# Score blocks of a slot on different rows of the array, P.V products in every second step, and exponentials in a ring of fifteen blocks

## The chip, the cores and the metric

The kernel runs on one core of one Trainium2 chip. The metric is the device time of one execution in microseconds (us), less is better. The median of three runs of the kernel before is 852.49 us (851.96 to 856.82).

## What is computed

A gated mix of two branches over the same 2048 tokens of width 640, all in bf16: softmax attention with 32 heads of width 20, and a dense layer with a Mish activation and 1536 hidden columns.

```python
g = sigmoid((x * gate_w).sum(-1, keepdims=True))

# branch A: attention, H = 32 heads, Dh = 20
qkv = (x @ wqkv).reshape(B, S, 3, H, Dh).transpose(2, 0, 3, 1, 4)
q, k, v = qkv[0], qkv[1], qkv[2]
p = softmax(einsum("bhqd,bhkd->bhqk", q, k) * Dh ** -0.5, axis=-1)
a = einsum("bhqk,bhkd->bhqd", p, v).transpose(0, 2, 1, 3).reshape(B, S, D) @ wo

# branch B: dense, Mish, dense
h = einsum("bsd,df->bsf", x, w1) + b1
sp = log1p(exp(-abs(h))) + where(h > 0, h, 0)
b = einsum("bsf,fd->bsd", h * tanh(sp), w2)

out = g * a + (1 - g) * b
```

## The kernel before

**Blocks.** The scores are computed transposed: keys on the partitions, 512 queries in the free direction. A *block* is one head's scores of 128 keys against 512 queries, one PSUM bank. Four heads with consecutive numbers form a head group `g` (there are 8) and lie on the 32-row strips `j` = 0 to 3 of `QT` and `KT`, so that score products of different `j` use different rows of the array (`tile_position=(32 * j, 0)`). With 4 chunks of queries `c` and 16 tiles of keys `kt` there are 4 x 8 x 16 x 4 = 2048 blocks. The last group is cut into two halves of 256 queries.

**Slots and steps.** A *slot* holds up to three blocks, in PSUM banks 0 to 2 (even slots) or 3 to 5 (odd ones). The main loop makes one *step* per slot. In step s ScalarE takes the exponential of slot s in one instruction (`emit_e`, L1086); then the scores of slot s + 2 are composed and emitted (`compose`, `emit_s`, `score_mms`, L1048), P.V products follow (`emit_pv`, `pv`, L1242), and last come *projections*: all products of the dense branch, of the QKV projection and of the output projection, taken from a list of tasks with due times (`pick`, `put`). Projections write to bank 7; when much of that work is owed (`now["rate"] > LEND`), odd slots hold only two blocks and lend bank 5 to projections as well (`lend`). The score products of slot s + 2 wait until slot s has been read.

**Blocks on VectorE.** Some slots carry an *extra*: their last block does not go to ScalarE. VectorE turns it into an approximate exponential in float16 bits, with a multiply and add that writes int16 (`emit_x`, L1117). The four heads of one key tile form a *tile* of four extras in four slots; when all four are in, VectorE makes three shifted copies (`SHADES`, L1137), and all four versions enter the P.V sum, so such a tile has four P.V sets in place of one. `choose` decides whether a slot gets an extra, by VectorE's backlog (`BEHIND`), by the fixed work that VectorE still owes (`room`, `LOAD`), and by free lines for the copies. `block_of` picks a block of the tile on a row that the slot's other two blocks don't use, if the tile has one left.

**P.V.** A *set* of P.V is the four heads of one key tile, four products of 21 columns side by side in the array (`tile_position=(0, 32 * j)`), summed in bank 6 over the whole group. `emit_pv` is called in each step and emits up to two sets of ScalarE blocks, and before each of them up to two sets of VectorE tiles (`emit_off`). When a group's last set is done, `group_done` copies the sum out and normalises it, and `hold` keeps P.V back for two steps.

**Where exponentials are kept.** `ETS` has five places (`NETS`) of three blocks (`SLOT`); slot s writes place s % 5, and waits for the P.V products of slot s - 5.

**What sets the order.** All five engines' instruction lists are written in one pass by a planner in the kernel's Python (`Plan`). It keeps an estimated time for each engine (`pl.now`), adds the cost given with each instruction (a change of the kind of product on TensorE adds `SWITCH`), and decides by these times; the constants at the top are its costs and thresholds. On the chip each engine runs its list in order, with semaphore waits between engines. A second program for inputs with very large scores follows behind a flag; it does not run with these inputs.

Of the kernel before, what the change touches and what calls it, by code (L numbers as in the profile page):

```python
# [13 lines left out]
AF = mybir.ActivationFunctionType  # L14
# [4 lines left out]
S = 2048  # L19
# [5 lines left out]
HG = 4  # L25
# [9 lines left out]
SCALE = DH ** -0.5  # L35
EW = DH + 1
NETS = 5
SLOT = 3
# [21 lines left out]
RECIP = 1.66  # L60
BLOCK = 0.43
STEP = 1.1
SLACK = 0.21
LATER = 0.616
FREE = 0.2
RISK = {"pe": 0.1, "act": 0.3, "dve": 0.5, "pool": 1.2, "sp": 0.6}
AHEAD = 16
BEHIND = 11.984
MORE = 5.931
PATIENCE = 1.785  # L70
CATCH_UP = 361.25
BUSY = 0.449
CROWD = 1.4
MARGIN = 0.575
EAGER = 26
LOAD = 0.786
MISH = 2.3
GROUP = 2.66
LAST = 0
OVER = 0.233  # L80
XSLACK = 0.336
BROAD = 1.13
LEND = 0.199
BEND = -0.21302449
QUART = (1.268632, -0.12838686 / 0.0119972, 0.72980421 / 0.0119972)
LEAD = 0.0119972
END = 83
SHIFT = 0.492
LAG = 200
WINDOW = 4.087  # L90
CALM = 4
PACKED = 13
Q_AT = 100
Q_STEP = 14.5
SQ = 25
SQ_STEP = 13
H_AT = 150
H_STEP = 12.5
# [122 lines left out]
def bass_gated_mix__softmax_full_mha__dense_activation_mish__prompt_kernel(  # L221
# [111 lines left out]
    def scores(s):  # L333
        return PS[:, SLOT * (s % 2):SLOT * (s % 2 + 1), :]

    NSLOT = -(-NC * NG * NKT * HG // SLOT)


# [3 lines left out]
    def attention(pl, fast):  # L342
# [7 lines left out]
        soon = deque()  # L350
        norm = deque()
        acts = deque()
        now = {"step": -1, "at": -2, "open": None, "home": FB, "bank": False, "rate": 9.0, "lent": False}


        if fast:
# [75 lines left out]
        def issue(task, bank):  # L432

            deps = []
            if task.done == 0:
                deps = [*task.ready(), bank_free.get(bank)]
            fn = task.mms[task.done]
            task.done += 1
            op = pl.add("pe", lambda e: fn(e, bank), deps, cost=task.cost)
            if task.done == len(task.mms):  # L440
                now["bank"] = True
                bank_free[bank] = task.finish(bank, op)
                now["bank"] = False
                return True
            return False
# [556 lines left out]


        s_op, e_op = {}, {}
        pv_slot, pv_left = {}, {}
        ev_op = {}
        taken, newest = set(), [-1]
        line_free = {("l", n): [] for n in range(LINES - fast)}
# [10 lines left out]
        def compose(s, extra=None):  # L1019

            n = SLOT - (s % 2 and now["lent"])
            if extra:
                slots[s] = [order.popleft() for _ in range(min(n - 1, len(order)))] + [extra]
            else:
                slots[s] = [order.popleft() for _ in range(min(n, len(order)))]
            now["at"] = (len(units) - len(order)) // SLOT - 2

        def emit_s(s):
# [9 lines left out]
        def score_mms(s, some, deps):  # L1038

            op = None  # L1040
            for r in range(max(len(subs(*u[:3])) for u in some)):
                began = False
                for i, (c, g, kt, j) in enumerate(some):
                    if r >= len(subs(c, g, kt)):
                        continue
                    tile, cols, of_q = subs(c, g, kt)[r]
                    cost = max(extent(c, g)[1] * COL, THIN)
                    op = pl.add("pe", lambda e, i=i, g=real(g), tile=tile, j=j, cols=cols, c=c, of_q=of_q: e.matmul(  # L1048
                        scores(s)[:, i, cols], KT[32 * j:32 * j + 32, g, tile * P:(tile + 1) * P],
                        QT[32 * j:32 * j + 32, g, c * CW:(c + 1) * CW][:, of_q], start=True, stop=True,  # L1050
                        tile_position=(32 * j, 0)), deps, cost=0.004 if began else cost, kind="S")
                    began, deps = True, []
            return op

        def repeat_s(s):
# [18 lines left out]
        def emit_e(s):  # L1074
            n = len(slots[s])
            by_dve = fast and s in off
            if by_dve:
                n -= 1
            while pv_left.get(s - NETS):

                hold["until"] = 0
                emit_pv(now["step"], 99)
                if pv_left[s - NETS]:
                    flush(lambda: emit_off(queue[0][2][:2], True, True))
                    emit_pv(now["step"], 99)
            e_op[s] = pl.add("act", lambda e: e.activation(  # L1086
                ETS[:, s % NETS, 0:n, :], scores(s)[:, 0:n, :], AF.Exp, scale=SCALE),
                [s_op[s], pv_slot.get(s - NETS)], cost=wide(s))
            pv_left[s] = n
            queue.extend((s, i, u) for i, u in enumerate(slots[s][:n]))  # L1090

# [68 lines left out]

        def choose(s, start):

            js = [v[3] for v in islice(order, 2)]
            late = max(0.0, pl.now["dve"] - pl.now["act"])
            urgent, other = (sum(t[0] for todo in some for t in todo) for some in ((norm, soon), (blend, bg)))
            tile = tile_now[0]
            if tile:
                if order and order[0][:2] == tile["key"][:2] and late + urgent + other >= BEHIND + MORE:
                    return None
                off[s] = block_of(tile, js)  # L1170
                return off[s][1]
            need = sum(len(SHADES) - len(t["items"]) for t in unshaded)
            if (not start or len(order) < 4 * HG or late + urgent + other >= BEHIND
                    or len(spare()) < 1 + min(need, len(SHADES) - 1)):
                return None
            c, g = group = order[2][:2]
            mine = [v for v in islice(order, 80) if v[:2] == group]
            left = (len(mine) - HG) * BLOCK
            before = sum(t[0] for t in blend if t[3] < pl.now["act"] + left)
            work_left = late + urgent + before + (len(SHADES) - 1) * SHADE  # L1180
            kts = [kt for kt in range(tiles(c, g)) if sum(v[2] == kt for v in islice(order, 2, 80) if v[:2] == group) == HG]
            if (len(kts) < 2 or 4 * EXP_PAIR + work_left * CROWD + MARGIN >= left
                    or newest[0] > place[group]):
                n = place[group] + 1
                if n >= len(groups):
                    return None
                c, g = group = groups[n]
                kts = [kt for kt in range(2) if (c, g, kt) not in taken]
                need = [k_done.get((real(g), 0)), q_done.get((real(g), c))]
                if not kts or any(op is None or safe(op) > pl.now["pe"] for op in need):  # L1190
                    return None
            key = (c, g, kts[0])
            taken.add(key)
            newest[0] = place[group]
            for j in range(HG):
                order.remove((*key, j))
            act_left[group] -= HG
            at, deps = grab()
            tile_now[0] = tile = {"key": key, "at": at, "deps": deps, "left": list(range(HG)), "seen": 0,
                                  "items": [], "given": 0, "shaded": None, "read": None}  # L1200
            off_tiles.setdefault(group, []).append(tile)
            off[s] = block_of(tile, js)
            return off[s][1]
# [41 lines left out]
                        cost=0.004 if n else max(w * COL, THIN), kind="V")  # L1245
            return lasts

        def emit_pv(step, passes):

            while passes and step >= hold["until"]:  # L1250
                if not queue:
                    return
                c, g, kt, _ = queue[0][2]
                emit_off((c, g), False)
                if len(queue) < HG:
                    return
                final = act_left[(c, g)] == HG
                if final and not emit_off((c, g), True):
                    if order or step + 1 in slots:
                        return  # L1260
                    flush(lambda: emit_off((c, g), True, True))
                passes -= 1
                some = [queue.popleft() for _ in range(HG)]
                lasts = pv([(u, ETS[:, s % NETS, i, :], [e_op[s]]) for s, i, u in some], final)
                act_left[(c, g)] -= HG
                for k, (s, i, u) in enumerate(some):
                    op = pv_slot[s] = lasts[k]
                    pv_left[s] -= 1
                if final:
                    hold["until"] = step + PV_HOLD  # L1270
                    group_done(c, g, step, op)
# [162 lines left out]
        def pick(limit):  # L1434
# [5 lines left out]
            begin = max(pl.now["pe"] + switch, free.t1 + HOP + FREE if free is not None else 0)  # L1440
            passed = False
            for t in tasks:
                if begin + t.cost > limit or passed and t.due > now["at"] + EAGER:
                    return None
                more = t.ready()
                passed = passed or more is None
# [81 lines left out]
        while True:  # L1528
# [41 lines left out]
                if fast and step + 2 in off:  # L1570
                    emit_x(step + 2)
            busy = order or step + 1 in slots
            emit_pv(step, 2 if busy else 99)

            limit = pl.now["act"] + wide(step + 1) + HOP + OVER if busy else 1e9
            owed = min(owed + rate, 1.0) if busy else 1e9
            while owed > 0:
                t = pick(limit)
# [180 lines left out]
```

## Time and profile before

| | |
|---|---|
| median of the runs | 852.49 us |
| profiled execution | 852.54 us, of which 850.2 us are the span from first to last instruction |
| TensorE matmuls (PE) | 832.1 us, 98% of the span |
| ScalarE (ACT) | 817.7 us, 96% |
| VectorE (DVE) | 701.8 us, 83% |
| TensorE weight loads (PEld) | 286.0 us, 34% |
| GpSimd (POOL) | 15.2 us, 2% |
| DMA | 42.58 MB, 50 GB/s on average |
| granted TensorE clock | 0.999 |

In the lines shown below, `L1086` is line 1086 of the kernel; `out<-in` are the program's names of the tiles written and read. A row of the groups of instructions ends with count, busy time and mean duration of one in ns, and, behind the last bar, the idle time of the engine ahead of them and what ended it. A row of the waits names who waited, for whom, the total in us, the number of times and the longest. A row in order of time begins with start and length in us and merges neighbours of one kind; its count is the number of instructions. A row of a stretch gives its length and each engine's busy time and, in brackets, count. Matmuls are pipelined, so the length of one is not what it adds to the time.

### The profile page before, as it was taken

The page shows a single profiled execution, that of the slowest core. Times are in us where ns is not written, and L with a number is a line of the kernel's source. Part 1 is how long each engine was busy: PE and PEld are TensorE (multiplying, and loading weights), DVE is VectorE, ACT ScalarE, POOL GpSimd, SP SyncE. Part 2 cuts the span into 40 slices and gives each one's busy share as a digit, 9 for nine tenths or more (in the row PEclk, how much of TensorE's full clock was granted, in tenths as well). Part 3 has the DMA queues.
Part 4 walks back from the last instruction along what each step waited for, and adds up shares of the span by engine and source line. Part 5 has one row for each costly group of instructions (what it writes and reads, how often), then busy time and mean ns, then how long its engine had stood idle before and what let it go on. Part 6 is the DMA issues. An engine that isn't in the chain of part 4 may idle for free.

```text
span 850.2 us, 17518 instructions
## 1 busy us (share of the span) xinstructions
PE 832.1 (98%) x7405; PEld 286.0 (34%) x7405; DVE 701.8 (83%) x1097; ACT 817.7 (96%) x848; POOL 15.2 (2%) x29
## 2 busy tenths in 40 slices
PE   8999999999999999999999999999999999999996
PEld 3333333233323333223333333333333333333332
DVE  4578776888798898987688999997999999998775
ACT  6999999999999999999999999999999999999995
POOL 3000000000000000000000000000000000000000
PEclk9999999999999999999999999999999999999999
DMA  9112110111112201131211121201112212000001
GB/s 216 40 52 52 58 38 3 35 55 48 30 55 81 62 31 42 33 106 41 48 50 48 51 72 43 64 22 37 47 58 60 77 39 74 17 26 25 15 15 35
DMA packets 70021, 42.58 MB, mean 50 GB/s; under 512 B 20616, under 2 KB 65920, under 8 KB 69888
## 3 DMA queue, kind: packets, MB, share of 16 engines
q1 hardware_dynamic: 67568, 40.89, 17.3%
q8 instruction: 61, 1.00, 0.5%
q10 hardware_dynamic: 2256, 0.47, 0.3%
q0 software_dynamic: 112, 0.01, 0.2%
q14 instruction: 24, 0.20, 0.1%
HBM read 33.97 MB, written 5.23 MB: 46 GB/s over the span
## 4 chain that ended last, share of the span: by engine, by line
PE 86%; ACT 10%; DMA 2%; SPq 1%; issue 0%; DVE 0%
PE PS L1048 32%; PE PS L1242 24%; ACT ETS L1086 9%; PE PS L901 7%; PE PS L840 7%; PE PS L547 5%; PE PS L925 4%; PE PS L722 2%; PE PS L601 2%; DMA XB<-in_A_x_dram 1%; SPq L478 1%; PE PS L763 1%; DMA REG<-in_B_w_dram 1%; PE PS L695 1%; PE PS L620 0%; ACT REG L874 0%
## 5 line engine op out<-in xcount | busy, mean ns | idle before, releaser
L1086 ACT ACTIVATE ETS<-PS 128x1024 bf16<-128x1024 f32 (+1 forms) x817 | 791.8, 1047 | 17.0 <-PE PS L1048 8.5
L1048 PE MATMUL PS<-QT,KT 32*128 32x512 bf16 (+1 forms) x2112 | 357.4, 377 | 6.6 <-ACT ETS L1086 5.3
L1117 DVE TENSOR_SCALAR LN<-PS 128x512 int16<-128x512 f32 x300 | 206.2, 687 | 72.8 <-PE PS L1048 68.4
L1242 PE MATMUL PS<-ETS,V_all 128*21 128x512 bf16 (+1 forms) x1720 | 163.7, 377 | 1.0 <-ACT ETS L1086 0.9
L1048 PEld LDWEIGHTS PS<-QT,KT 32*128 32x128 bf16 x2112 | 81.7, 91 | 230.6 <-ACT ETS L1086 130.5
L1137 DVE TENSOR_SCALAR LN<-LN 128x2048 int16<-128x2048 int16 x183 | 122.4, 684 | 0.5
L1242 PE MATMUL PS<-LN,V_all 128*21 128x512 f16 (+1 forms) x1300 | 111.8, 377 | 0.0
L901 PE MATMUL PS<-W2R,HB 128*128 128x320 bf16 x384 | 76.9, 303 | 0.0
L1242 PEld LDWEIGHTS PS<-ETS,V_all 128*21 128x21 bf16 x1720 | 42.1, 89 | 73.7 <-issue 64.3
L840 PE MATMUL PS<-XB,REG 128*128 128x256 bf16 x360 | 58.1, 275 | 0.4 <-DMA REG<-in_B_w_dram 0.4
L925 PE MATMUL PS<-WOQ,QT 128*128 128x320 bf16 x256 | 52.4, 303 | 0.0
L547 PE MATMUL PS<-XB,WOQ 128*128 128x512 bf16 x155 | 49.1, 384 | 0.0
L901 PEld LDWEIGHTS PS<-W2R,HB 128*128 128x128 bf16 x384 | 30.0, 97 | 44.7 <-issue 38.8
L1242 PEld LDWEIGHTS PS<-LN,V_all 128*21 128x21 bf16 x1300 | 25.9, 89 | 52.9 <-issue 27.8
L840 PEld LDWEIGHTS PS<-XB,REG 128*128 128x128 bf16 x360 | 28.6, 97 | 30.0 <-issue 26.4
L1117 DVE TENSOR_SCALAR REG<-PS 128x512 int16<-128x512 f32 x44 | 30.2, 686 | 7.5 <-PE PS L1048 6.7
L850 DVE TENSOR_TENSOR HB<-PS,B1F 128x512 bf16<-128x512 f32 x48 | 32.8, 684 | 2.9 <-PE PS L840 2.8
L925 PEld LDWEIGHTS PS<-WOQ,QT 128*128 128x128 bf16 x256 | 20.2, 97 | 29.6 <-issue 25.3
L893 DVE SCALAR_TENSOR_TENSOR U<-U 128x1024 f32<-128x1024 f32 x24 | 29.0, 1210 | 0.0
L559 DVE CAST QT<-PS 128x512 bf16<-128x512 f32 x31 | 21.3, 686 | 7.6 <-PE PS L547 7.2
L722 PE MATMUL PS<-REG,XB 128*128 128x160 bf16 (+1 forms) x240 | 26.0, 234 | 0.0
L1313 DVE COPY OUNG<-PS 128x512 f32<-128x512 f32 x31 | 21.3, 687 | 5.2 <-PE PS L1242 5.1
(113 smaller groups left out, 525.9 us busy)
## 6 DMA issues: line engine op xcount, KB each, us to landing
REG<-in_B_w_dram SPq DMA_DIRECT2D x36, 320.0 KB, 3.2
BCT<-SUMS SPq DMA_DIRECT2D x31, 256.0 KB
W2R<-in_B_w_dram SPq DMA_DIRECT2D x12, 320.0 KB, 4.7
KT<-KS SPq DMA_DIRECT2D x28, 128.0 KB
KS<-LN SPq DMA_DIRECT2D x16, 128.0 KB, 1.7
W2R<-in_B_w_dram SPq DMA_DIRECT2D x1, 1920.0 KB, 9.9
out_dram<-REG SPq DMA_DIRECT2D x24, 80.0 KB, 1.6
REG<-in_A_wqkv_dram SPq DMA_DIRECT2D x2, 700.0 KB, 8.3
```

What stands on the lines that cost most here:

```text
L547: return lambda e, bank: e.matmul(PS[:, bank, :], pads[:, b, f, :], xt(c)[:, f, :], start=(f == 0), stop=(f == NFT - 1))
L722: return lambda e, bank: e.matmul(PS[:, bank, i * n:(i + 1) * n], xt(t // 4)[:, f, t % 4 * P:(t % 4 + 1) * P], WV[:, f, g * HD:g * HD + n] ...
L840: return lambda e, bank: e.matmul(PS[:, bank, i * HW:(i + 1) * HW], w1b(n1)[:, f, i * P:(i + 1) * P], xt(c)[:, f, cols], start=(f == 0), s ...
L850: ev = dve(lambda e: e.tensor_tensor(hb, PS[:, bank, :].rearrange("p (i t) -> p i t", i=2), bias, ALU.add), [last, *b1f, *guarded, *b_read ...
L893: piece(BROAD, lambda e: e.scalar_tensor_tensor(G, G, b, G, ALU.add, ALU.mult))
L901: return lambda e, bank: e.matmul(PS[:, bank, 0:HALF], HB[:, hc % 2, f, t * P:(t + 1) * P], W2[:, f, half * HALF:(half + 1) * HALF], start ...
L925: return lambda e, bank: e.matmul(PS[:, bank, 0:HALF], otn(c, g)[:, t * P:(t + 1) * P], WOG[:, g, half * HALF:(half + 1) * HALF], start=(g ...
L1048: op = pl.add("pe", lambda e, i=i, g=real(g), tile=tile, j=j, cols=cols, c=c, of_q=of_q: e.matmul(scores(s)[:, i, cols], KT[32 * j:32 * j ...
L1086: e_op[s] = pl.add("act", lambda e: e.activation(ETS[:, s % NETS, 0:n, :], scores(s)[:, 0:n, :], AF.Exp, scale=SCALE), [s_op[s], pv_slot.g ...
L1117: ev_op[s] = tile["op"] = dve(lambda e: e.tensor_scalar(dst, scores(s)[:, 2, :], SCALE * ULPS, BASE, ALU.mult, ALU.add), [s_op[s], *tile[" ...
L1137: op = pl.add("dve", lambda e: e.tensor_scalar(to, src, SHADES[n], None, ALU.add), [last, *deps], cost=SHADE)
L1242: lasts[n] = pl.add("pe", lambda e, tile=tile, h=real(g) * HG + j, j=j, src=src[:, cols], of_q=of_q, begin=begin, end=end: e.matmul(PS[32 ...
```

## The change

- `compose` fills a slot block by block: an extra is placed first, and each next block is one from the first key tile of `order` that lies on a row not yet used in the slot, if there is one. The extra still comes last in the slot. `choose` tells `block_of` the rows of all blocks that remain of the first key tile, or none if more than two remain.
- Exponentials are written to a ring (`RING`, the same memory as `ETS`, 15 blocks); a slot takes as many blocks as it has, and waits for the P.V products of whichever slots own these blocks.
- `emit_pv` is called only in odd steps (`TURN`), unless `tight` holds (one of the next `ROOM` blocks of the ring is still unread, the oldest set is the group's last, or nothing else is to come) or `VMIN` sets are ready. Unless `tight`, it stops at the planner's `limit` for the step.
- A projection that begins a piece needs `FMIN` of room; each projection product is costed `MORE_MM` higher.
- Constants of the planner have other values.

```diff
-SLACK = 0.21
-LATER = 0.616
+SLACK = 0.225
+LATER = 0.659
-BEHIND = 11.984
+BEHIND = 44.659
-PATIENCE = 1.785
-CATCH_UP = 361.25
-BUSY = 0.449
+PATIENCE = 2.856
+CATCH_UP = 413.595
+BUSY = 0.437
-EAGER = 26
-LOAD = 0.786
+EAGER = 62
+LOAD = 1.258
-GROUP = 2.66
+GROUP = 2.418
-LEND = 0.199
+FMIN = 0.25
+VMIN = 11.592
+ROOM = 4.229
+TURN = 1
+MORE_MM = 0.005
+LEND = 0.139
-END = 83
-SHIFT = 0.492
-LAG = 200
+END = 33
+SHIFT = 0.481
+LAG = 186
-CALM = 4
+CALM = 10
-SQ = 25
+SQ = 32
...
+    NRING = NETS * SLOT
+    RING = ETS[:, :, :, :].rearrange("p a b c -> p (a b) c")
...
-        op = pl.add("pe", lambda e: fn(e, bank), deps, cost=task.cost)
+        op = pl.add("pe", lambda e: fn(e, bank), deps, cost=task.cost + MORE_MM)
...
         def compose(s, extra=None):
             n = SLOT - (s % 2 and now["lent"])
-            if extra:
-                slots[s] = [order.popleft() for _ in range(min(n - 1, len(order)))] + [extra]
-            else:
-                slots[s] = [order.popleft() for _ in range(min(n, len(order)))]
+            some = [extra] if extra else []
+            while len(some) < n and order:
+                js = [u[3] for u in some]
+                mates = [u for u in islice(order, HG) if u[:3] == order[0][:3]]
+                u = next((u for u in mates if u[3] not in js), mates[0])
+                order.remove(u)
+                some.append(u)
+            slots[s] = some[1:] + some[:1] if extra else some
...
         def emit_e(s):
-            while pv_left.get(s - NETS):
+            p = now["ring"] if now["ring"] + n <= NRING else 0
+            before = {owner.get(i) for i in range(p, p + n)} - {None}
+            while any(pv_left[b] for b in before):
                 hold["until"] = 0
                 emit_pv(now["step"], 99)
...
             e_op[s] = pl.add("act", lambda e: e.activation(
-                ETS[:, s % NETS, 0:n, :], scores(s)[:, 0:n, :], AF.Exp, scale=SCALE),
-                [s_op[s], pv_slot.get(s - NETS)], cost=wide(s))
+                RING[:, p:p + n, :], scores(s)[:, 0:n, :], AF.Exp, scale=SCALE),
+                [s_op[s], *(pv_slot[b] for b in before)], cost=wide(s))
+            spot[s] = p
+            owner.update({i: s for i in range(p, p + n)})
+            now["ring"] = (p + n) % NRING
...
         def choose(s, start):
-            js = [v[3] for v in islice(order, 2)]
+            js = [v[3] for v in islice(order, HG) if v[:3] == order[0][:3]]
+            if len(js) > 2:
+                js = []
...
+        def pressed():
+            at = now["ring"]
+            return any(pv_left.get(owner.get((at + i) % NRING)) for i in range(int(ROOM)))
+
-        def emit_pv(step, passes):
-            while passes and step >= hold["until"]:
+        def emit_pv(step, passes, limit=1e9):
+            while passes and step >= hold["until"] and pl.now["pe"] + PASS <= limit:
...
             for t in tasks:
-                if begin + t.cost > limit or passed and t.due > now["at"] + EAGER:
+                if begin + (t.cost if pl.kind == "F" else max(t.cost, FMIN)) > limit or passed and t.due > now["at"] + EAGER:
                     return None
...
             busy = order or step + 1 in slots
-            emit_pv(step, 2 if busy else 99)
             limit = pl.now["act"] + wide(step + 1) + HOP + OVER if busy else 1e9
+            tight = not fast or not busy or pressed() or queue and act_left[queue[0][2][:2]] == HG <= len(queue)
+            if tight or step % 2 == TURN or sets() >= VMIN:
+                emit_pv(step, 2 if busy else 99, 1e9 if tight else limit)
```

More of the change, by code (lines that the diff above doesn't have):

```diff
@@ L352, in attention @@
         acts = deque()
-        now = {"step": -1, "at": -2, "open": None, "home": FB, "bank": False, "rate": 9.0, "lent": False}
+        now = {"step": -1, "at": -2, "open": None, "home": FB, "bank": False, "rate": 9.0, "lent": False, "ring": 0}
         if fast:
@@ L1004, in attention @@
         s_op, e_op = {}, {}
-        pv_slot, pv_left = {}, {}
+        pv_slot, pv_left, spot, owner = {}, {}, {}, {}
         ev_op = {}
@@ L1041, in score_mms @@
             for r in range(max(len(subs(*u[:3])) for u in some)):
-                began = False
+                rows = set()
                 for i, (c, g, kt, j) in enumerate(some):
@@ L1050, in score_mms @@
                         QT[32 * j:32 * j + 32, g, c * CW:(c + 1) * CW][:, of_q], start=True, stop=True,
-                        tile_position=(32 * j, 0)), deps, cost=0.004 if began else cost, kind="S")
-                    began, deps = True, []
+                        tile_position=(32 * j, 0)), deps, cost=0.004 if rows and j not in rows else cost, kind="S")
+                    rows.add(j)
+                    deps = []
             return op
@@ L1078, in emit_e @@
                 n -= 1
-            while pv_left.get(s - NETS):
+            p = now["ring"] if now["ring"] + n <= NRING else 0
+            before = {owner.get(i) for i in range(p, p + n)} - {None}
+            while any(pv_left[b] for b in before):
                 hold["until"] = 0
                 emit_pv(now["step"], 99)
-                if pv_left[s - NETS]:
+                if any(pv_left[b] for b in before):
                     flush(lambda: emit_off(queue[0][2][:2], True, True))
@@ L1246, in pv, with sets @@
             return lasts
-        def emit_pv(step, passes):
-            while passes and step >= hold["until"]:
+        def sets():
+            if not queue:
+                return 0
+            n = len(queue) // HG
+            for tile in off_tiles.get(queue[0][2][:2], ()):
+                n += sum(op.t1 + HOP <= pl.now["pe"] for op, _ in tile["items"][tile["given"]:])
+            return n
+        def pressed():
[3 more added lines that the diff above has]
+            while passes and step >= hold["until"] and pl.now["pe"] + PASS <= limit:
                 if not queue:
@@ L1263, in emit_pv @@
                 some = [queue.popleft() for _ in range(HG)]
-                lasts = pv([(u, ETS[:, s % NETS, i, :], [e_op[s]]) for s, i, u in some], final)
+                lasts = pv([(u, RING[:, spot[s] + i, :], [e_op[s]]) for s, i, u in some], final)
                 act_left[(c, g)] -= HG
```

## Prediction

> **What bounds the kernel now.** I read the page's header first, then the waits, then ScalarE's and TensorE's instructions in order of time.
>
> ```profile
> span 850.2 us, 17518 instructions
> PE 832.1 (98%) x7405; PEld 286.0 (34%) x7405; DVE 701.8 (83%) x1097; ACT 817.7 (96%) x848; POOL 15.2 (2%) x29
> PE 86%; ACT 10%; DMA 2%; SPq 1%; issue 0%; DVE 0%
> PEld PS L1048 <- ACT ETS L1086: 130.5, 346, 0.9
> DVE LN L1117 <- PE PS L1048: 68.4, 112, 2.0
> ACT ETS L1086 <- PE PS L1048: 8.5, 34, 1.1
> PE PS L1048 <- ACT ETS L1086: 5.3, 21, 0.5
> ```
>
> Two engines look full, TensorE at 98% and ScalarE at 96%. The chain of work that ended last (third line) runs 86% on TensorE, but a busy share can hide waiting inside. The waits (last four) say that TensorE's score matmuls stood still for ScalarE only 5.3 us in all; the 130.5 us of the first are the weight loads, which are issued ahead and wait in the shadow of running matmuls. VectorE waits for TensorE's scores. To see who waits in truth, take the exponentials one by one:
>
> ```profile
> L1086 ACT ACTIVATE ETS<-PS 128x1024 bf16<-128x1024 f32 x783 | 748.9, 1028 | 16.5 <-PE PS L1048 8.0 <-PE PS L1242 1.1
> L1086 ACT ACTIVATE ETS<-PS 128x1536 bf16<-128x1536 f32 x34 | 48.8, 1466 | 0.5 <-PE PS L1048 0.5
> L874 ACT ACTIVATE REG<-HB,MXR 128x1024 f32<-128x1024 bf16 x18 | 20.6, 1144 | 0.0
> L874 ACT ACTIVATE W2R<-HB,MXR 128x1024 f32<-128x1024 bf16 x6 | 6.9, 1146 | 0.0
> ...
> 10.27 4.13 ACT L1086 ACTIVATE ETS<-PS 128x1536 bf16<-128x1536 f32 x3 [0.49 <-PE PS L1048]
> 369.22 6.52 ACT L1086 ACTIVATE ETS<-PS 128x1024 bf16<-128x1024 f32 x7
> 371.04 4.70 ACT L1086 ACTIVATE ETS<-PS 128x1024 bf16<-128x1024 f32 x5
> 298.46 21.65 ACT L1086 ACTIVATE ETS<-PS 128x1024 bf16<-128x1024 f32 x22
> 834.65 6.43 ACT L1086 ACTIVATE ETS<-PS 128x1536 bf16<-128x1536 f32 x5
> ```
>
> An exponential of two blocks lasts 1.028 us (mean), but its successor starts before it ends. The rows at 369.22 and 371.04 end together and differ by two exponentials and 1.82 us: 0.91 us from start to start. The row at 298.46 has 22 in 21.65 us: (21.65 - 1.03) / 21 = 0.98. ScalarE is seen busy all that time, yet runs 7% under its pace: the wait is shorter than the overlap, so no idle time is recorded. Three blocks take (4.13 - 1.47) / 2 = 1.33. So ScalarE's own work, packed tight, is 783 x 0.91 + 34 x 1.33 + 27.5 (Mish, L874) = 785 us; with 10.3 us ahead of the first exponential and 9.1 after the last (834.65 + 6.43 = 841.1, span 850.2) that is **804 us**. It has about 46 us of slack.
>
> TensorE has none. A piece of its order:
>
> ```profile
> 301.05 0.39 PE L1048 MATMUL PS<-QT,KT 32*128 32x512 bf16 x3
> 301.38 0.40 PE L1242 MATMUL PS<-W2R,V_all 128*21 128x512 f16 x4
> 301.60 0.39 PE L1242 MATMUL PS<-ETS,V_all 128*21 128x512 bf16 x4
> 301.92 0.39 PE L1048 MATMUL PS<-QT,KT 32*128 32x512 bf16 x2
> 302.24 0.61 PE L620 MATMUL PS<-XB,REG 128*48 128x512 bf16 x3
> ...
> 304.95 0.60 PE L1048 MATMUL PS<-QT,KT 32*128 32x512 bf16 x3
> 305.48 0.40 PE L1242 MATMUL PS<-ETS,V_all 128*21 128x512 bf16 x4
> 305.81 0.38 PE L722 MATMUL PS<-REG,XB 128*128 128x161 bf16 x3
> 306.13 0.39 PE L1048 MATMUL PS<-QT,KT 32*128 32x512 bf16 x2
> ```
>
> Starts are to be compared, not lengths. Two P.V sets in a row are 0.22 apart (301.38 to 301.60). Whenever the kind of product changes, scores to P.V (301.05 to 301.38) or P.V to scores (301.60 to 301.92), it is 0.32-0.33: a change of kind costs **0.10 us**. The slot at 304.95 lasts 0.60 against 0.39 at 301.05, and its follower starts 0.53 later, not 0.32: two of its three blocks lie on the same 32 rows, so one runs after the other, **0.21 us** more. Nothing in this stretch waits. TensorE's order sets the time.
>
> **The change part by part.** *Rows.* Such doubled slots are long from first to last:
>
> ```profile
> 24.43 0.60 PE L1048 MATMUL PS<-QT,KT 32*128 32x512 bf16 x3
> 808.64 0.60 PE L1048 MATMUL PS<-QT,KT 32*128 32x512 bf16 x3
> L1117 DVE TENSOR_SCALAR LN<-PS 128x512 int16<-128x512 f32 x300 | 206.2, 687 | 72.8 <-PE PS L1048 68.4
> L1117 DVE TENSOR_SCALAR REG<-PS 128x512 int16<-128x512 f32 x44 | 30.2, 686 | 7.5 <-PE PS L1048 6.7
> L1117 DVE TENSOR_SCALAR HB<-PS 128x512 int16<-128x512 f32 x24 | 16.5, 689 | 8.8 <-PE PS L1048 8.5
> L1117 DVE TENSOR_SCALAR W2R<-PS 128x512 int16<-128x512 f32 x12 | 8.2, 687 | 3.2 <-PE PS L1048 3.2
> ```
>
> The first and the last of 182, among 383 three-block slots. 300 + 44 + 24 + 12 = 380 blocks go to VectorE (95 tiles), one in a slot, and it is this extra block that doubles: `choose` avoids the two ScalarE blocks' rows only while the tile has others left, so half are caught. All 182 gone is 182 x 0.21 = 38 us. The new order can still be caught: with four or three blocks of the key tile left in `order` a mate on another row always exists; with two left both must be taken and two of the tile's four extras meet them; with one left, one of four. Were the four cases equally frequent, (0 + 0 + 2 + 1) / 16 = 19% would stay, 74 of some 390, and the gain is 108 x 0.21 = 23. I take the middle, 40 left: **-30 us**, bounds -23 and -38.
>
> *P.V in every second step.*
>
> ```profile
> 13.44 0.40 PE L1242 MATMUL PS<-ETS,V_all 128*21 128x512 bf16 x4
> 839.48 0.71 PE L1242 MATMUL PS<-ETS,V_all 128*21 128x256 bf16 x9
> 20.33 0.32 PE L695 MATMUL PS<-REG,XB 128*128 128x80 bf16 x4
> 829.28 0.31 PE L925 MATMUL PS<-WOQ,QT 128*128 128x320 bf16 x1
> ```
>
> Between the first two, P.V comes in 504 unbroken pieces, in 817 steps (783 + 34 exponentials). With odd steps alone there are about 408, plus one for each of the 32 groups' ends, say 440: 64 pieces fewer. A piece removed between scores and projections saves one change of kind, between scores and scores two; 230 of 504 stand before scores, so 1.46 changes, 0.15 us: **-10 us**. Bounds: all 96 at two changes, -20; and +3 if `limit` cuts pieces so that 20 more arise. The sets themselves (0.22 each) remain. `FMIN` forbids starting a projection piece with under 0.25 us of room; I cost it at nothing, as the matmul comes in the next piece, though joining the 116 shortest pieces (0.25 to 0.35 us, the last two rows are the first and the last) could give up to 116 x 0.10 = 12.
>
> *The ring.* The exponential gains no instruction; its wait for old P.V sets changes from five slots (ten blocks with pairs) to fifteen blocks. Behind a waiting exponential stand all later ones and the Mish on ScalarE, and through the score banks TensorE; a P.V product postponed by one step holds two more blocks, five more fit. I take 0; from below one wait of a P.V pass per group end, 32 x 0.2 = +6.
>
> *Constants.*
>
> ```profile
> L1137 DVE TENSOR_SCALAR LN<-LN 128x2048 int16<-128x2048 int16 x183 | 122.4, 684 | 0.5
> L893 DVE SCALAR_TENSOR_TENSOR U<-U 128x1024 f32<-128x1024 f32 x24 | 29.0, 1210 | 0.0
> 750.00:800.00 50.00, 50.00 (x429) 15.80 (x426) 42.71 (x68) 49.00 (x52) 0.00 (x0) 1.00 0.07 22
> ```
>
> `BEHIND` 12 to 45 and `LOAD` let VectorE take a tile with a longer backlog; `CALM` 10 starts it later. Nearly every odd slot already lends its third bank, so even slots, 408 of 817, are the ceiling: 102 tiles against 95. Each tile more takes 4 x 0.42 us off ScalarE (1.33 - 0.91), adds three P.V sets, 3 x 0.22, on TensorE, and 4 x 0.687 + 3 x 0.684 = 4.8 us on VectorE, which has 148 us free. I take four tiles: **+3 us** on TensorE (0 to +5), -7 on ScalarE. `END` 83 to 33 only spreads projections; TensorE is full in the last stretch too (50.00 of 50.00 us).
>
> Sum: -30 - 10 + 3 = **-37**. The profiled execution took 852.5 us (2.3 around the span), which is the median of the runs as well: 815.5. ScalarE would need 804 - 7 = 797 + 2 = 799 by itself. With the two only 2% apart they trip over each other more often than now; for 5.3 us of TensorE's waiting at 6% distance I add 2: **817 us**.
>
> **Rivals.** *ScalarE is the bound* (or the planner hands the freed time out as waiting). For: 96% busy. Then only its recorded waits for scores go, 8.5 us: 844 to 852. Against: 0.91 against 0.98. The Trainium skill, "Perfetto Trace Analysis", section "Identifying the Most-Contended Engine", speaks for this rival: TensorE's headroom is not to be read from matmul busy time but from weight-load share and arithmetic. Here the weight loads are busy 34%, which by that rule leaves TensorE far from its limit, and ScalarE would be the engine to relieve. The trace has the loads hidden under row- and column-tiled matmuls and the 0.10 us changes of kind in neither figure, so I hold to the starts.
>
> *Half of it.* Extras are still caught in 74 slots, P.V pieces stay at about 500 because ring pressure or group ends break the alternation: -23 + 3 + 2 = -18, 834. For: `tight` bypasses the alternation whenever one of the next four ring blocks is unread.
>
> *VectorE becomes the late one* (slower). For: the larger backlog lets four-block tiles in while Mish pieces (1.2 us each) queue on an in-order engine; TensorE's scores two steps on wait for the VectorE read of the same bank (`ev_op`). Price: d us at each of about 395 extras. At d = 0.10 the 37 us are eaten; at half a VectorE read (0.34) for half of them, 198 x 0.34 = 67 us and the time is 852 - 37 + 67 = 882. Against: VectorE now waits for scores, 68.4 us, and not the reverse.
>
> *More than forecast.* No doubled slot left, all 96 pieces gone, 12 us of joined projections: -38 - 20 - 12 + 3 = -67, but ScalarE's 799 stops it: 799 to 801, less only if more blocks leave ScalarE.
>
> **How the numbers follow.** Forecast (801 to 830) 0.60; half of it (830 to 844) 0.18; no change 0.08; VectorE late, slower, 0.06; under 801, 0.08. The bounds of the sum itself, -23 + 3 + 6 + 5 = -9 to -67, reach over all but the last two. The range 797 to 840 leaves out half of the under-801 case, a third of the half case and both bad ones, about 0.2. One per cent, about what a measurement can tell from no change, is 844 to 861: faster 0.86, same 0.08, slower 0.06.
>
> **What would show it.** In the profile after: score slots of 0.60 fall from 182 to under 80; P.V pieces fall from 504 to about 440, more of them with two or three sets; exponentials of two blocks run at 0.92 to 0.95 from start to start and ScalarE's idle share shrinks little; TensorE's matmuls wait more for ScalarE (5.3 us now) or are still full; VectorE's reads stay at 380 to 410 and wait less for scores. The prediction is wrong if scores wait for VectorE's reads (a row that does not exist now), if ScalarE waits for P.V at the ring, or if doubled slots persist above 100.

## The result

The changed kernel takes 817.27 us (median of 4 runs, 815.89 to 819.0) against 854.43 us of the kernel before in the same session: ratio 0.9566, 95% interval 0.9524 to 0.9609, 37 us less. The forecast was 817 in a range of 797 to 840. The profiled execution took 815.99 us, of which 813.5 are the span. Below, "at a like clock" refers to the granted TensorE clock of each run: the kernel before takes about 7 us more for each 0.01 less of it (851.98 us at 1.000, 858.44 at 0.991).

The header of the changed kernel's page, the chain of work that ended last, and the waits of TensorE's and ScalarE's score work:

```profile
span 813.5 us, 17511 instructions
PE 780.5 (96%) x7377; PEld 280.5 (34%) x7418; DVE 697.4 (86%) x1104; ACT 794.1 (98%) x849; POOL 15.4 (2%) x29
ACT 75%; PE 17%; DMA 3%; DVE 2%; SPq 1%; issue 0%; ACTq 0%
PE PS L1060 <- ACT ETS L1101: 12.4, 41, 1.0
ACT ETS L1101 <- PE PS L1060: 3.3, 6, 1.0
DVE LN L1135 <- PE PS L1060: 52.1, 78, 2.3
PE PS L1060 <- DVE LN L1135: 0.6, 1, 0.6
```

In the chain that ended last the two full engines have changed places: it was 86% TensorE and is 75% ScalarE; TensorE's score products now wait for ScalarE 12.4 us (5.3 before), ScalarE for scores 3.3 (8.5 before). VectorE still waits for scores and is waited for once, 0.6 us.

ScalarE's groups, and its exponentials in order of time:

```profile
L1101 ACT ACTIVATE ETS<-PS 128x1024 bf16<-128x1024 f32 x790 | 736.0, 1092 | 2.9 <-PE PS L1060 2.4
L1101 ACT ACTIVATE ETS<-PS 128x1536 bf16<-128x1536 f32 x28 | 41.7, 1504 | 0.9 <-PE PS L1060 0.9
L882 ACT ACTIVATE REG<-HB,MXR 128x1024 f32<-128x1024 bf16 x18 | 21.5, 1195 | 0.0
L882 ACT ACTIVATE W2R<-HB,MXR 128x1024 f32<-128x1024 bf16 x6 | 7.2, 1202 | 0.0
...
297.70 12.23 ACT L1101 ACTIVATE ETS<-PS 128x1024 bf16<-128x1024 f32 x13
482.21 14.98 ACT L1101 ACTIVATE ETS<-PS 128x1024 bf16<-128x1024 f32 x16
794.27 10.06 ACT L1101 ACTIVATE ETS<-PS 128x1024 bf16<-128x1024 f32 x9 [0.68 <-PE PS L1060]
```

Start to start they now take (12.23 - 1.09) / 12 = 0.93 and (14.98 - 1.09) / 15 = 0.93 us, where the stretch at the same place before took 0.98; over the whole traces the mean distance of two-block exponentials is 0.97 us before and 0.93 after. The mean length of one has grown, from 1028 to 1092 ns, while the pace rose, so here the length of an instruction is no measure of the pace. ScalarE's own work by the prediction's reckoning, 790 x 0.91 + 28 x 1.33 + 28.7 (Mish) + 10.4 ahead of the first + 9.2 after the last (794.27 + 10.06 = 804.3), is again 804 us. It has not become shorter; its hidden waiting went from 46 us to some 10. (The commonest distance in the whole changed trace is 0.904 us, so 0.91 makes ScalarE's own work some 5 us too long, in both kernels alike.)

TensorE in order of time, near the stretch shown of before, then the first and the last doubled slot and the first and the last P.V piece:

```profile
301.05 0.39 PE L1060 MATMUL PS<-QT,KT 32*128 32x512 bf16 x3
301.37 0.59 PE L730 MATMUL PS<-REG,XB 128*128 128x161 bf16 x6
301.90 0.39 PE L1060 MATMUL PS<-QT,KT 32*128 32x512 bf16 x2
302.22 0.40 PE L1262 MATMUL PS<-W2R,V_all 128*21 128x512 f16 x4
302.44 0.39 PE L1262 MATMUL PS<-LN,V_all 128*21 128x512 f16 x4
302.66 0.39 PE L1262 MATMUL PS<-ETS,V_all 128*21 128x512 bf16 x4
302.98 0.39 PE L1060 MATMUL PS<-QT,KT 32*128 32x512 bf16 x3
...
168.63 0.60 PE L1060 MATMUL PS<-QT,KT 32*128 32x512 bf16 x3
709.52 0.60 PE L1060 MATMUL PS<-QT,KT 32*128 32x512 bf16 x3
13.53 0.40 PE L1262 MATMUL PS<-ETS,V_all 128*21 128x512 bf16 x4
803.23 0.63 PE L1262 MATMUL PS<-ETS,V_all 128*21 128x256 bf16 x10
```

The alternation is plain to see: a step with projections alone (301.37), then one with three P.V sets in a piece (302.22 to 302.98) and no projection. Doubled slots are 21 of 381 (182 of 383 before), P.V pieces 409 (504). Projection pieces are 552 (578): this trace lacks 41 of the 7418 matmuls, so pieces and changes of kind are counted from the weight loads, of which none is missing and which come in the same order.

### The profile page after: what moved, and what is told of

It is laid out like the page before. It is cut to its first block, busy times and chain, and to the rows that moved or that the text cites. A ratio compares the mean times of both kernels' runs of the same rounds, so it can differ in the third digit from the quotient of the medians.

```text
span 813.5 us, 17511 instructions
## 1 busy us (share of the span) xinstructions
PE 780.5 (96%) x7377; PEld 280.5 (34%) x7418; DVE 697.4 (86%) x1104; ACT 794.1 (98%) x849; POOL 15.4 (2%) x29
## 4 chain that ended last, share of the span: by engine, by line
ACT 75%; PE 17%; DMA 3%; DVE 2%; SPq 1%; issue 0%; ACTq 0%
ACT ETS L1101 73%; PE PS L1060 6%; PE PS L1262 4%; ACT REG L882 2%; PE PS L555 2%; DMA XB<-in_A_x_dram 1%; PE PS L848 1%; SPq L486 1%; PE PS L730 1%; PE PS L609 1%; DMA BCT<-SUMS 1%; PE PS L933 1%; DMA SUMS<-RR 1%; DMA RR<-OUNG 1%; DVE LN L1135 1%
## 5 line engine op out<-in xcount | busy, mean ns | idle before, releaser
L1101 ACT ACTIVATE ETS<-PS 128x1024 bf16<-128x1024 f32 (+1 forms) x818 | 769.7, 1106 | 3.8 <-PE PS L1060 3.3
L1060 PE MATMUL PS<-QT,KT 32*128 32x512 bf16 (+1 forms) x2112 | 323.2, 378 | 17.1 <-ACT ETS L1101 12.4
L1135 DVE TENSOR_SCALAR LN<-PS 128x512 int16<-128x512 f32 x316 | 216.9, 686 | 55.5 <-PE PS L1060 52.1
L1060 PEld LDWEIGHTS PS<-QT,KT 32*128 32x128 bf16 x2112 | 79.2, 91 | 254.0 <-ACT ETS L1101 222.6
L1155 DVE TENSOR_SCALAR LN<-LN 128x2048 int16<-128x2048 int16 x187 | 125.4, 684 | 1.1 <-PE PS L1262 0.5
L1262 PE MATMUL PS<-LN,V_all 128*21 128x512 f16 (+1 forms) x1296 | 107.2, 376 | 1.1 <-DVE LN L1135 1.1
L933 PE MATMUL PS<-WOQ,QT 128*128 128x320 bf16 x256 | 50.5, 302 | 0.2 <-DVE QT L1340 0.2
L555 PE MATMUL PS<-XB,WOQ 128*128 128x512 bf16 x132 | 41.0, 383 | 2.1 <-issue 2.1
L909 PEld LDWEIGHTS PS<-W2R,HB 128*128 128x128 bf16 x384 | 28.7, 97 | 35.7 <-issue 30.3
L1262 PEld LDWEIGHTS PS<-LN,V_all 128*21 128x21 bf16 x1296 | 24.1, 89 | 42.7 <-issue 26.4
L1135 DVE TENSOR_SCALAR REG<-PS 128x512 int16<-128x512 f32 x40 | 27.4, 686 | 7.4 <-PE PS L1060 7.1
```

The source lines that it names most:

```text
L555: return lambda e, bank: e.matmul(PS[:, bank, :], pads[:, b, f, :], xt(c)[:, f, :], start=(f == 0), stop=(f == NFT - 1))
L909: return lambda e, bank: e.matmul(PS[:, bank, 0:HALF], HB[:, hc % 2, f, t * P:(t + 1) * P], W2[:, f, half * HALF:(half + 1) * HALF], start ...
L933: return lambda e, bank: e.matmul(PS[:, bank, 0:HALF], otn(c, g)[:, t * P:(t + 1) * P], WOG[:, g, half * HALF:(half + 1) * HALF], start=(g ...
L1101: e_op[s] = pl.add("act", lambda e: e.activation(RING[:, p:p + n, :], scores(s)[:, 0:n, :], AF.Exp, scale=SCALE), [s_op[s], *(pv_slot[b] f ...
L1135: ev_op[s] = tile["op"] = dve(lambda e: e.tensor_scalar(dst, scores(s)[:, 2, :], SCALE * ULPS, BASE, ALU.mult, ALU.add), [s_op[s], *tile[" ...
L1155: op = pl.add("dve", lambda e: e.tensor_scalar(to, src, SHADES[n], None, ALU.add), [last, *deps], cost=SHADE)
```

## The experiments

Each kernel was timed beside the kernel before; ratios are to that, and what is lost or gained against the changed kernel is the difference of two ratios. 0.01 is 8.5 us. The edits are shown shortened. Where the planner's decisions change, the whole order is made anew, so part of a difference is another plan; I give the counts that show it.

**Does TensorE set the time before, and ScalarE after?** Two kernels with less to do on ScalarE; the weight loads of both come in exactly the order of the kernel they start from (in the changed kernel the edit is the same with `RING`):

```diff
-ETS[:, s % NETS, 0:n, :], scores(s)[:, 0:n, :], AF.Exp
+ETS[:, s % NETS, 0:n, 0:448], scores(s)[:, 0:n, 0:448], AF.Exp
```

> The kernel before with exponentials of 448 of each block's 512 columns (the other 64 columns are left out and stay zero); the planner's costs and so the order stay. ScalarE has 1668 blocks x 64 columns less, about 87 us. Theory 1 (TensorE's order set the time before): 843 to 853. Theory 2 (ScalarE did): 790 to 815.

> The changed kernel with exponentials of 448 of each block's 512 columns (the other 64 columns are left out and stay zero), 87 us less on ScalarE, order unchanged. Theory 1 (ScalarE sets the time now, and TensorE's own order needs 55 us less than before): the time falls to TensorE's own length, 790 to 802. If TensorE's order still sets it: 810 to 817.

Before: 0.9948 (0.9917 to 0.998), 4 us for 87 us of ScalarE's work. After: 0.9459 (0.9424 to 0.9494), 809.5 us, 9 us below the changed kernel; the range I had written, 790 to 802, was missed. The header and chain of the changed kernel with short exponentials:

```profile
span 806.0 us, 17553 instructions
PE 786.6 (98%) x7418; PEld 281.3 (35%) x7418; DVE 694.7 (86%) x1105; ACT 749.5 (93%) x849; POOL 15.4 (2%) x29
PE 81%; DVE 8%; DMA 5%; ACT 4%; SPq 1%; issue 0%
ACT ETS L1103 <- PE PS L1062: 30.9, 134, 2.0
```

The chain returns to TensorE, and ScalarE waits for scores openly, 30.9 us. So TensorE's own order needs at most about 809 us after the change, and the two engines lie close together. The counterpart, 204 small ScalarE instructions more, in every fourth step:

```diff
+if fast and s % 4 == 2:
+    pl.add("act", lambda e: e.activation(DUM[:, 0:192], DUM[:, 192:384], AF.Exp), [m_dum], cost=0.0)
```

> The kernel before with a ScalarE instruction more in every fourth step (204 of them, an exponential of 192 columns in SBUF, about 0.2 us each, 41 us in all), at no cost in the planner, so the order of everything else stays. Theory 1 (TensorE's order sets the time, ScalarE has about 46 to 57 us of hidden slack): 853 to 868. Theory 2 (ScalarE sets it): 885 to 895.

> The same 204 ScalarE instructions in the changed kernel. Theory 1 (ScalarE is the engine that sets the time now): about 41 us less half of the 22 us of slack, 840 to 858. Theory 2 (TensorE still sets it): 817 to 830.

The group of exponentials and two rows in order of time, of the changed kernel with them:

```profile
L1104 ACT ACTIVATE ETS<-PS 128x1024 bf16<-128x1024 f32 x790 | 778.3, 1198 | 2.7 <-PE PS L1063 2.6
303.51 0.48 ACT L1111 ACTIVATE DUM<-DUM 128x192 bf16<-128x192 bf16 x1
303.76 3.88 ACT L1104 ACTIVATE ETS<-PS 128x1024 bf16<-128x1024 f32 x4
```

One takes 0.25 us from start to start, 204 x 0.25 = 51 us, not 41. Before: 1.0114 (1.0051 to 1.0177), +10 us, so 41 of 51 vanished in the slack reckoned at 46; there the chain is already 67% ScalarE. After: 1.0057 (1.0036 to 1.0079) instead of 0.9566, +42 us, so 9 vanished. Both speak for theory 1; the upper end I had written for the kernel after, 858, was passed (860.56), as the probe was a quarter larger than planned.

**The same on TensorE**, one score product made twice in every fourth step:

```diff
+if fast and s % 4 == 2:
+    s_op[s] = pl.add("pe", lambda e: e.matmul(scores(s)[:, 0, :], ...same operands as block 0...), [], cost=0.0, kind="S")
```

> The kernel before with one score product of the slot made twice in every fourth step (204, 0.21 us each, 43 us on TensorE, no change of kind), at no cost in the planner, so that the order of everything else stays. Theory 1 (TensorE sets the time): 885 to 898. Theory 2 (ScalarE sets it): 852 to 865.

> The same in the changed kernel, 202 products, 43 us on TensorE. Theory 1 (ScalarE sets the time now, TensorE waits some 19 us for it more than before): 835 to 848. If TensorE still sets it: 855 to 862.

Before: 1.0274 (1.0216 to 1.0333), +23 us; after: 0.9902 (0.9867 to 0.9937), 848.75 us, +29 us. The first, 881.0 us, lies between the two ranges I had written; the second is just past theory 1's 848 and short of the other's 855. In order of time, in the kernel before with the probe:

```profile
305.37 0.39 PE L1056 MATMUL PS<-QT,KT 32*128 32x512 bf16 x2
305.60 0.37 PE L1041 MATMUL PS<-QT,KT 32*128 32x512 bf16 x1
305.60 0.37 PE L1056 MATMUL PS<-QT,KT 32*128 32x512 bf16 x1
305.90 0.40 PE L1250 MATMUL PS<-LN,V_all 128*21 128x512 f16 x4
```

The added product (L1041) runs beside the doubled extra (L1056 at the same 305.60): where the extra is late on another row, the repetition is free. Of 191 full slots with the probe that can be told apart in the trace, only 20 need two passes more, 171 one, though about 90 were doubled already: some 70 repetitions cost nothing, and 204 - 70 = 134 x 0.21 = 28 us were really added. Against those, 23 us is nearly all. In the changed kernel 189 of 189 take one pass more, 42 us were added, and 29 came through. So each engine, when it gets more to do, lengthens the changed kernel: ScalarE by 42 of 51 us, TensorE by 29 of 42.

**The rows alone**, and the change without them (in the second, only `compose` and `choose` go back):

```diff
 rows_only: kernel before
+compose, choose and the cost by row of the changed kernel
 no_rows: changed kernel
-js = [v[3] for v in islice(order, HG) if v[:3] == order[0][:3]] ...
+js = [v[3] for v in islice(order, 2)]
 (and compose as before)
```

> The kernel before with the new filling of slots alone (compose, choose, and the planner's cost of a score product by its row). Theory 1, TensorE's order set the time before and the doubled slots are the larger part: 182 of them fall below 60, 26 to 38 us leave TensorE, the time falls to 816 to 828. Theory 2, ScalarE set the time and the gain came from the constants and the P.V steps: 845 to 853.

> The changed kernel with the old filling of slots; everything else stays, the planner's cost by row too. Theory 1: some 190 doubled slots come back, 40 us on TensorE; ScalarE's slack of 22 us in the changed kernel hides little of it: 838 to 852. Theory 2: 812 to 824, as now.

Alone: 0.98 (0.974 to 0.986), 837.3 us, 17 us less: neither range (19 to 20 us less at a like clock: 833.21 at 0.999 against 852.08 at 0.999). Without: 0.9933 (0.9909 to 0.9958), 849.15 us, 31 us of the 37 lost, as theory 1 has it; 162 doubled slots are back, (162 - 21) x 0.21 = 30 us. (This plan also gives VectorE 360 blocks instead of 384, 10 us more for ScalarE, so that the loss is not the passes' alone.) Alone the rows take 182 doubled slots down to 36, worth 146 x 0.21 = 31 us, and a third to a half of that is lost again. ScalarE's waits in the kernel with the rows alone point to one cause:

```profile
ACT ETS L1091 <- PE PS L1249: 9.8, 6, 3.2
ACT ETS L1091 <- PE PS L1052: 5.1, 12, 1.4
```

The first is new: exponentials wait for P.V products (L1249), 9.8 us in six waits of up to 3.2, where the kernel before had 1.1 us. An exponential waits for a P.V product only because its place is still unread, so the five places run out there; that the faster scores are the reason is my reading and was not tested. The plan also gives VectorE 372 blocks in place of 380, 8 x 0.42 = 3 us of ScalarE. Together 31 - 10 - 3 = 18; that the three simply add up is not shown.

**The ring, and the alternation.**

```diff
 five_places: changed kernel
-p = now["ring"] if now["ring"] + n <= NRING else 0
+p = s % NETS * SLOT
-now["ring"] = (p + n) % NRING
+now["ring"] = (p + SLOT) % NRING
 every_step: changed kernel
-if tight or step % 2 == TURN or sets() >= VMIN:
-    emit_pv(step, 2 if busy else 99, 1e9 if tight else limit)
+emit_pv(step, 2 if busy else 99)
```

> The changed kernel with exponentials in five places of three blocks, as before the change, and P.V still in odd steps. Theory 1 (the ring only gives room for postponed P.V): the ring pressure breaks the alternation in more steps, P.V pieces rise from 409 to 430 to 480, 3 to 12 us: 820 to 829. Theory 2 (the ring takes a wait of ScalarE away): ScalarE waits for P.V at the places, 830 or more. Neither: 815 to 819.

> The changed kernel with P.V called in each step, without limit. Theory 1: some 95 pieces of P.V more, each 0.15 to 0.2 us in changes of kind, 14 to 19 us on TensorE, which now waits for ScalarE some 20 us more than before and hides part: 822 to 833. Theory 2 (TensorE's work is hidden behind ScalarE now): 815 to 820.

Five places: 0.9783 (0.9727 to 0.9838), 837.45 us, 19 us lost, the rival's side of what I had written. P.V pieces stay at 409, so the alternation does not break; ScalarE waits:

```profile
ACT ETS L1101 <- PE PS L1262: 6.4, 17, 0.5
ACT ETS L1101 <- PE PS L1060: 6.3, 10, 1.3
```

The first row does not exist in the changed kernel. These are the recorded parts; summing what each exponential's start lies beyond its pace, and looking which product ended just before it, gives 13.5 us of waiting for P.V in 47 exponentials (none in the changed kernel). The remade plan has 58 doubled slots instead of 21, 37 x 0.21 = 8 us of TensorE, and 368 blocks for VectorE instead of 384, 16 x 0.42 = 7 of ScalarE.

Without the alternation: 0.9819 (0.9774 to 0.9864), 838.98 us, 22 us lost, more than theory 1's range. But part of that is the clock: the run of the median had 0.982 granted, where the kernel before had 0.991 to 1.000 in twelve of thirteen runs beside it, and this kernel too gets longer with a lower clock (834.79 us at 0.989, 840.3 at 0.980). At a like clock it would take some 830 us by my estimate, which leaves 11 to 13 lost and lies inside theory 1's range; why the clock was lower is open. From its profiled execution, at a clock of 0.967, I take only counts. P.V pieces 501 against 409, 92 x 0.15 = 14 us; doubled slots 43 against 21, 5 us; VectorE 368 blocks, 7 us of ScalarE.

So rows alone and rows with alternation both stand at 837, rows with ring at 839 (some 830 at a like clock), ring and alternation without the rows at 849; only the three together reach 817. The first of these has the old constants, the others the new. The alternation holds exponentials longer, and the 13.5 us with five places show that it then needs the ring. The ring alone, and the alternation alone, were not run.

**The constants, and the planner's knowledge.**

```diff
 old_constants: changed kernel
+every constant that the kernel before has, with its old value
 told: kernel before
-cost=0.004 if began else cost
+cost=0.004 if rows and j not in rows else cost
```

> All code of the change with the constants of before (those that are new keep their values). It plans 372 blocks for VectorE against 384, five ScalarE us more. Theory 1 (rows, ring and alternation together are the gain): 817 to 828. Rival (the gain hangs on the constants): 835 to 852.

> The kernel before with the planner's cost of a score product by its row alone: the planner knows of the doubled slots and plans round them, but they stay. Theory 1 (the passes themselves cost): 848 to 858. Rival (the planner's wrong times cost, and right ones give part of the gain): 825 to 843.

Old constants: 0.966 (0.9625 to 0.9696), 828.83 us, just past theory 1's range: the constants are worth some 8 us of the 37. Two counts go with it, and which of them it is was not separated: VectorE has 372 blocks instead of 384, 12 x 0.42 = 5 us of ScalarE, and 52 slots are doubled instead of 21, 31 x 0.21 = 6.5 us of TensorE. Told (the changed kernel has this line too): 1.0082 (1.0049 to 1.0115), 862.85 us, past the upper end of theory 1, 858, with 173 doubled slots and 368 blocks for VectorE. Its clocks were lower, mostly 0.985 to 0.987 against 0.991 to 0.999 beside it, and by the 7 us for 0.01 that would account for about the 6 us. So no loss is shown, and no gain: a right estimate alone, without the new filling of the slots, brought nothing.

## Why the prediction was right

- *What bounds it.* Right. ScalarE's 87 us less moved the kernel before by 4 us, and 51 us more by 10. Reading starts instead of lengths showed a slack of 46 us behind a busy share of 96%; the probe found at least 41.
- *Rows.* -30 with 40 doubled slots left; 21 are left, 161 x 0.21 = -34. Taken away from the whole they cost 31. The case analysis gave 0 to 74, and the middle was too cautious.
- *P.V in every second step.* -10 with 440 pieces; 409 came, and with the projections' 26 fewer pieces all changes of kind fell from 1887 to 1768, 119 x 0.10 = -12.
- *The ring.* Costed at 0 as an addition; no exponential of the changed kernel waits for P.V. But I missed that without it the alternation would not pay: 19 us are lost. What I had as "five more fit" was the condition for the term of the alternation.
- *Constants.* Four tiles more were taken, one came, 384 blocks for 380. That term was +3 on TensorE and is +0.6; -7 on ScalarE, and is -2. Yet the old values cost 8 us when put back: what else the constants do to the plan, the doubled slots among it, was not in the sum.
- *The sum.* -34 - 12 + 0.6 = -45 by counts; by the run with short exponentials TensorE's own order shrank from 852 to 809.5, -43. I had -37, 815.5. The term that was mis-sized on the other side is the last, "they trip over each other, 2 us": the changed kernel is 8 to 9 us above TensorE's own order and, with 804 + 2.5, 11 above ScalarE's. Two errors of 6 us cancelled; that the forecast was good to the microsecond was luck, its sign and its rough size were not.
- *Rivals.* "ScalarE is the bound" fell for the kernel before and is half true of the one after. The rule of the Trainium skill ("Perfetto Trace Analysis", "Identifying the Most-Contended Engine") would, as far as weight loads go, have sent a reader to ScalarE; its other measure, arithmetic, was not worked out here. The trace does not bear it out: weight loads are busy 34% before and 34% after, while the time fell by 4.3% with ScalarE's own work at 804 us as before. Here the starts of the matmuls, and the probes, decide. "VectorE late" did not come: scores waited for its reads once, 0.6 us, though its busy share rose to 86%. By the letter this row is one of the signs of being wrong that the prediction names; at that size it moves nothing. "Half of it" is about where the rows end when one of the other two is missing.

What stays open: how much of the 20 us that each single withdrawal costs is the edit and how much the plan remade around it. The counts above come near the measured losses, but they mix time of TensorE with time of ScalarE, and the constants were not fitted anew for any variant.

## What to carry to other kernels

Two engines can show 98% and 96% and only one be full: compare the distance of starts with the shortest distance that the same instruction reaches anywhere in the trace, and confirm with a probe that adds 5% to one engine without touching the order. On a full matrix engine, count two things that no busy share shows, products of one group that fall on the same rows (one pass each) and changes between kinds of product (0.10 us each here). When the bound is taken away, look which buffer the next engine waits for: an edit that was reckoned at nothing by itself, here the ring, may be the condition for the one that pays.

## What was not expected of the hardware

- A product repeated on a row that is done runs beside a later one on another row, with the same start (305.60 and 305.60): a doubled slot leaves room on the other rows, and some 70 repetitions used it without cost.
- The recorded length of an exponential grew from 1028 to 1092 ns, while the mean distance to the next fell from 0.97 to 0.93 us; with the added ScalarE instructions it is 1198 ns. In these traces it is longer the fuller ScalarE is.
- An exponential of 192 columns, SBUF to SBUF, took 0.25 us from start to start, when 0.2 was planned.
